# Top-k attention feeding a SoLU MLP on one core: constant rows and a tenth query tile in place of six small VectorE operations of a step, with a new table of places

## The chip, the core and the metric

The kernel runs on one core of a Trainium2 chip. Its engines are called PE (TensorE, the matmuls), DVE (VectorE), ACT (ScalarE), POOL (GpSimd) and SP (SyncE, which here only issues DMAs). Each engine works through its own instructions in order and waits on semaphores for the others. The metric is the device time of one execution in microseconds. A program is run several times; its time is the median. One execution is also taken by the profiler, and every row shown below comes from that one.

## The reference

Inputs are q, k and v of 8 batches x 8 heads x 576 positions x 64 columns, and the weights of an MLP (512 to 1024 to 512). For every query row only the scores that are at least as large as the 32nd largest of the row enter the softmax:

```python
scores = scale * np.matmul(q, k.transpose(0, 1, 3, 2))
kth = np.partition(scores, -top_k, axis=-1)[..., -top_k:-top_k + 1]
scores = np.where(scores >= kth, scores, -1000000000.0)
attn = np.exp(scores - max);  attn = attn / (sum(attn) + 1e-09)
x = (attn @ v), heads side by side: 4608 tokens x 512
h = x @ w_in
solu = h * softmax(h)
ln = (solu - mean) / sqrt(var + 1e-06) * g_ln
out = ln @ w_out
```

## The kernel before, in words

There are 32 steps, four for each batch. A step takes nine query tiles of 128 rows (`NT = 9`): four chunks with two heads each make tiles 0 to 7, and the last 64 positions of two heads together make tile 8. Groups of three tiles (`NG = 3`) share some small operations. For each tile the kernel finds the 32nd largest score by guessing thresholds. `spread` multiplies the queries with the second moments of the keys on PE; `spread_v` (L821 to L835) multiplies that with the queries on DVE and scales the means; `spread_r` adds it up to the expected spread of each row; `first_p` on POOL takes the square root and makes the gain `tb`; `first` makes the first threshold `t0`. `count0` counts the scores above it (DVE, two of nine on ACT in the first four steps), `second` moves the threshold, `count1` counts again (ACT; from the fifth step on tiles 7 and 8 on DVE), `third` moves it once more, and `count2` (ACT) leaves signs. `side`, `nearest`, `best` and `kth` (DVE) find the exact 32nd value among the eight nearest ones; `exps` is on ACT; `keep` (DVE, L1025) applies the mask and sums the row; `inverse` (L1030 to L1036) makes 1/sum for a group of three tiles; `norm` (POOL, L1040) scales the row by it. PE then transposes the tile (`transpose_p`), ACT copies it out of PSUM (`copy_p`), and `attn_v` multiplies with the values.

The MLP of a 128-token tile (a token) is spread over later steps: `mm1` (PE), `hexp` (ACT), `solu` (DVE), `square` (ACT), `ln` (POOL), `transpose_ln` (PE), `copy_ln` (ACT), `mm2` (PE), `store` (ACT copy, then a DMA from SP). Every eight steps there is one more token made of the tails of two batches.

The small operations that matter here. `moved` (L914 to L934) changes a threshold by (count + a) * `tb` * part + old. The two constants differ between tiles counted on DVE and tiles counted on ACT, so a step with both kinds issues four small operations: two of L926, two of L931. `spread_v` does each of its two operations twice, since tile 8 lies in another place of PSUM than tiles 0 to 7: L830 on 512 and on 64 columns, L833 on 8 and on 1. `inverse` adds 1e-9 (L1033) and then takes the reciprocal (L1036), three times in a step.

PSUM tiles called `big` hold scores, `spread`'s result (`y_ps`) and `mm1`'s result (`h_ps`); there are two such buffers, used in turn. The queries of a step lie in one buffer (`qm`), the keys' and queries' tails in two (`qk_tails`, in turn).

The order is written out by hand. Every piece of work gets a time in a table (`step_times` for step i at 39 i plus the entry, `early_times` for the first four steps, `key_times`, tables for tokens and weights), all pieces are sorted by it, and each engine and SP's DMA queue then follow that order. The numbers are places, not measured times: a step is 39 units of the table long.

At the start the MLP's weights come as 64-bit floats and are converted by DVE, ACT and POOL (`w_bits`, `w_low`, `w_mul`, `w_add`). Their exponents are checked again from a second load (`w_again`, `w_exp` on DVE, `w_check` on ACT); `w_passed` (L1218) adds up all checks, and `w_verdict` (L1225 to L1228) makes one flag, which every engine reads before it branches over a general version of the kernel.

Of the kernel before, what the change touches and what calls it, by code (L numbers as in the profile page):

```python
# [15 lines left out]
P = 128  # L16
# [427 lines left out]
def fast_path(  # L444
# [96 lines left out]
    g_rows = const.tile([NF, P], F32, tag="g_rows", name="g_rows")  # L541
    g_col = const.tile([P, NF], F32, tag="g_col", name="g_col")

    ok = const.tile([P, 6], F32, tag="ok", name="ok")
# [3 lines left out]
    qk_tails = [const.tile([P, 2, P], F32, tag=f"qk_tails{n}", name="qk_tails") for n in range(2)]  # L548
    v_diag = [const.tile([P, P], F32, tag=f"v_diag{n}", name="v_diag") for n in range(4)]
    for t in qk_tails + v_diag:  # L550
        nc.vector.memset(t, 0.0)
# [27 lines left out]
    def load_g():  # L579
        nc.sync.dma_start(out=g_rows, in_=moe_g_ln.rearrange("(c p) -> c p", p=P))  # L580
        tp = ps_tp.tile([P, NM, P], F32, tag="tp", name="tp_g")
        nc.tensor.transpose(tp[:, 0, 0:NF], g_rows, ident[0:NF, 0:NF])
        nc.scalar.copy(out=g_col, in_=tp[:, 0, 0:NF])
# [89 lines left out]
    def load_k(n):  # L673
# [9 lines left out]
        d["tails"] = qk_tails[n % 2]  # L683
        for h in range(2):
            hd = slice(h * ST, (h + 1) * ST)
            nc.sync.dma_start(out=d["tails"][hd, 0, hd], in_=q[b, 2 * hp + h, SM:S, :])
        nc.sync.dma_start(
            out=d["tails"][0:ST, 1, :].rearrange("p (h d) -> p h d", h=2),
# [29 lines left out]
    def prep_t(n):  # L718

        for m in range(2):  # L720
            nc.tensor.transpose(
                pre_of(n)[:, m * P : (m + 1) * P], ks[n]["tails"][:, m, :], ident
            )
# [44 lines left out]
    def load_q(i):  # L768
        b, chunks = steps[i]
        d = st[i]  # L770
        d["q"] = p1.tile([P, NT, D], F32, tag="qm", name="qm")
# [28 lines left out]
    def spread(i):  # L800
# [3 lines left out]
        d["ym"] = y[:, :, 0 : NM * (D + 1)].rearrange("p h (t e) -> p t h e", e=D + 1)  # L804
        d["yt"] = y[:, 0, NM * (D + 1) : (NM + 1) * (D + 1)]
        for c in range(NM):
            for h in range(2):
                hd = slice(h * D, (h + 1) * D)
                nc.tensor.matmul(
                    out=d["ym"][:, c, h, :], lhsT=trunc(queries_of(i, c)[hd, :]),  # L810
                    rhs=trunc(keys_of(i, c)["mom"][hd, :]), start=True, stop=True,
                )
        nc.tensor.matmul(
            out=d["yt"], lhsT=trunc(queries_of(i, NM)), rhs=trunc(keys_of(i, NM)["mom"]),
            start=True, stop=True,
        )

    def spread_v(i):
        d = st[i]
        ym, yt, q9 = d["ym"], d["yt"], d["q"]  # L820
        yq = d["yq"] = p2.tile([P, NT, D], F32, tag="w", name="yq")  # L821
        d["mean"] = small.tile([P, NT], F32, tag="mean", name="mean")
        for o, y, qq, mean in (
            (yq[:, 0 : 2 * NM, :].rearrange("p (t h) d -> p t h d", h=2), ym,
             q9[:, 0 : 2 * NM, :].rearrange("p (t h) d -> p t h d", h=2),
             d["mean"][:, 0 : 2 * NM].rearrange("p (t h) -> p t h", h=2)),
            (yq[:, 2 * NM, :], yt, q9[:, 2 * NM, :], d["mean"][:, 2 * NM : NT]),
        ):
            main = len(y.shape) == 4
            nc.vector.tensor_tensor(  # L830
                out=o, in0=y[:, :, :, 0:D] if main else y[:, 0:D], in1=qq, op=ALU.mult
            )
            nc.vector.tensor_scalar(  # L833
                out=mean, in0=y[:, :, :, D] if main else y[:, D : D + 1],
                scalar1=scale / SM, scalar2=None, op0=ALU.mult,  # L835
            )

    def spread_r(i):
        d = st[i]
        d["ss"] = small.tile([P, NT], F32, tag="ss", name="ss")  # L840
        nc.vector.tensor_reduce(out=d["ss"], in_=d["yq"], axis=AX.X, op=ALU.add)

    def first_p(i):
# [10 lines left out]
        )  # L854

    def first(i):
        d = st[i]
        d["t0"] = small.tile([P, NT], F32, tag="t0", name="t0")
        nc.vector.tensor_tensor(out=d["t0"], in0=d["mean"], in1=d["zs"], op=ALU.add)
# [81 lines left out]
    def third(i):  # L941

        n = NT - n1_of(i)
        moved(i, "n1", "t1", "t2", [(slice(0, n), -513.0, -0.25), (slice(n, NT), -31.5, 0.5)])
        d = st[i]
        t2 = d["t2"]
# [83 lines left out]
    def inverse(i, g):  # L1030
        js = slice(3 * g, 3 * g + 3)
        rden = columns(i, "rden")[:, js]
        nc.vector.tensor_scalar(  # L1033
            out=rden, in0=den_all[:, i, js], scalar1=1e-9, scalar2=None, op0=ALU.add
        )
        nc.vector.reciprocal(rden, rden)  # L1036
# [201 lines left out]
    def at(time, f, *args):  # L1238
# [4 lines left out]
        (load_q, [()], [-52.3]),  # L1243
        (prep_q, [()], [-25.66]),
        (prep_qc, [()], [-21.32]),
        (spread, [()], [-14.74]),
        (spread_v, [()], [-12.28]),
        (spread_r, [()], [-9.11]),
        (first_p, [()], [-5.94]),
        (first, [()], [-3.94]),  # L1250
        (scores, range(5), [-7.74, -5.46, -3.54, 0.79, 4.68]),
        (evac, range(9), [-4.99, -4.94, -2.71, -2.43, -0.91, -0.66, 1.75, 4.87, 8.58]),
        (count0, range(9), [-3.49, -3.39, -1.8, -1.65, 1.1, 2.22, 6.88, 7.72, 8.66]),
        (count1, range(9), [13.91, 15.21, 12.34, 15.17, 15.19, 16.89, 17.13, 16.96, 21.1]),
        (count2, range(9), [29.61, 24.17, 28.68, 23.34, 23.78, 23.94, 47.62, 27.29, 29.63]),
        (second, [()], [11]),
        (third, [()], [22.2]),
        (exps, range(5), [52.85, 51.89, 50.14, 56.99, 57.42]),
        (side, range(3), [37.21, 28.03, 49.2]),
        (inverse, range(3), [62.57, 64.96, 71.31]),  # L1260
        (count_off, [()], [50.83]),
        (kth, [()], [59.45]),
        (nearest, range(9), [41.07, 47.51, 39.3, 32.69, 29.76, 32.16, 57.74, 55.76, 51.21]),
        (best, range(9), [46.43, 52.3, 45.06, 36.45, 31.16, 33.82, 59.19, 58.14, 52.97]),
        (keep, range(9), [60.36, 61.34, 60.51, 62.49, 61.26, 61.16, 68.47, 62.8, 65.92]),
        (norm, range(9), [66.71, 64.69, 67.66, 72.59, 68.38, 72.61, 76.63, 77.78, 82.81]),
        (transpose_p, range(9), [
            70.08, 67.75, 72.27, 74.68, 72.98, 77.69, 79.24, 81.24, 83.57,
        ]),
        (copy_p, range(8), [71.1, 70.74, 73.88, 77.75, 75.87, 78.46, 81.22, 82.02]),  # L1270
        (copy_pt, [()], [84.44]),
        (transpose_last, range(2), [85.94, 86.48]),
        (copy_last, range(2), [87.65, 89.55]),
        (attn_v, range(2), [87.9, 90.3]),
        (copy_v, range(2), [90.37, 92.29]),
# [4 lines left out]
            (load_q, [()], [-111.2]),  # L1280
            (prep_q, [()], [-67.51]),
            (prep_qc, [()], [-54.3]),
            (spread, [()], [-19.53]),
            (spread_v, [()], [-17.76]),
            (spread_r, [()], [-17.34]),
            (first_p, [()], [-5.49]),
            (first, [()], [-3.33]),
            (scores, range(5), [-19.43, -18.9, -12.69, -4.58, 0.75]),
            (evac, range(9), [-15.83, -10.83, -8.96, -7.82, -7.17, -3.89, 2.47, 1.78, 4.92]),
            (count0, range(9), [4, -2, 3.06, 6.67, -2.83, -2.66, 5.03, 4.47, 9.4]),  # L1290
# [349 lines left out]
```

## Time and profile before

| what | us |
|---|---|
| median of 3 runs | 1291.85 (1290.74 to 1292.61) |
| the profiled execution's own time | 1289.73 |
| its span, first to last instruction | 1287.8 |
| PE busy in the span | 1184.2 |
| DVE busy | 1148.7 |
| ACT busy | 1130.6 |
| POOL busy | 481.1 |

The page of the profile has six parts; the first two give the busy time of each engine in all and in 40 equal slices of the span. A group row names a line, the engine, the tiles, the shape and the count, then the busy time in all and the mean of one in ns. A timeline row has a start, a duration and an instruction. The window view gives the busy time of each engine in a stretch.

`spread_r`, once in a step, marks the steps: in the trace it starts at 566.2, 601.3, 636.4, 671.5, 710.1, 746.5 and 788.2 us. Before the sixth one the steps are 23.7 to 41.2 us long, and from the eighth on the pattern 35.1 five times, then 38.6, 36.4 and 41.8, comes back.

### The profile page before, as it was taken

The page shows a single profiled execution, that of the slowest core. Times are in us where ns is not written, and L with a number is a line of the kernel's source. Part 1 is how long each engine was busy: PE and PEld are TensorE (multiplying, and loading weights), DVE is VectorE, ACT ScalarE, POOL GpSimd, SP SyncE. Part 2 cuts the span into 40 slices and gives each one's busy share as a digit, 9 for nine tenths or more (in the row PEclk, how much of TensorE's full clock was granted, in tenths as well). Part 3 has the DMA queues.
Part 4 walks back from the last instruction along what each step waited for, and adds up shares of the span by engine and source line. Part 5 has one row for each costly group of instructions (what it writes and reads, how often), then busy time and mean ns, then how long its engine had stood idle before and what let it go on. Part 6 is the DMA issues. An engine that isn't in the chain of part 4 may idle for free.

```text
span 1287.8 us, 19758 instructions
## 1 busy us (share of the span) xinstructions
PE 1184.2 (92%) x5955; PEld 672.1 (52%) x5955; DVE 1148.7 (89%) x2916; ACT 1130.6 (88%) x2478; POOL 481.1 (37%) x583
## 2 busy tenths in 40 slices
PE   6556789999999999999999999999999999998996
PEld 3334355555555555555555555555555555554543
DVE  5999989999999988999999988999999997999612
ACT  3989987999999989999999889999999889998634
POOL 5544533443432324444432234444333233443310
PEclk9668899999999999999999999999999999999998
DMA  7301111011111021011110011101110101102311
GB/s 224 98 26 38 52 33 42 19 31 37 39 37 27 20 55 38 27 31 29 47 37 23 24 46 37 37 22 32 51 37 18 31 25 39 30 7 74 131 58 61
DMA packets 106756, 56.97 MB, mean 44 GB/s; under 512 B 89736, under 2 KB 97936, under 8 KB 106640
## 3 DMA queue, kind: packets, MB, share of 16 engines
q1 hardware_dynamic: 106640, 55.61, 15.6%
q8 instruction: 50, 0.82, 0.3%
q14 instruction: 66, 0.54, 0.1%
HBM read 46.14 MB, written 9.44 MB: 43 GB/s over the span
## 4 chain that ended last, share of the span: by engine, by line
PE 44%; ACT 29%; DVE 19%; issue 4%; POOL 2%; DMA 1%; SPq 0%; DVEq 0%; ACTq 0%; POOLq 0%
PE s_ps L883 12%; PE o_ps L1199 10%; PE h_ps L1141 7%; PE tp_p L1054 7%; ACT junka L908 7%; ACT sg L960 6%; DVE E L1025 5%; DVE junkv L900 5%; ACT E L996 4%; DVE w L988 3%; PE om L1111 3%; ACT PT L1067 3%; DVE w L981 3%; PE tp_ln L1188 2%; ACT X L892 2%
## 5 line engine op out<-in xcount | busy, mean ns | idle before, releaser
L1199 PE MATMUL o_ps<-w_out,lnT 128*128 128x512 f32 x576 | 260.7, 596 | 0.0
L1040 POOL TENSOR_SCALAR E<-E,rden 128x576 f32<-128x576 f32 x256 | 204.2, 811 | 106.7 <-DVE rden L1036 80.2
L900 DVE TENSOR_SCALAR_CACHE_REDUCE junkv<-X,t 128x576 bf16<-128x576 f32 x280 | 224.3, 801 | 14.8 <-ACT X L892 6.6
L953 POOL TENSOR_SCALAR tt<-t 128x9 f32<-128x9 f32 x32 | 19.8, 619 | 561.7 <-DVE t L948 561.3
L1141 PE MATMUL h_ps<-w_in,xTm 128*128 128x512 f32 x512 | 226.8, 595 | 0.3 <-ACT xTm L1127 0.3
L883 PE MATMUL s_ps<-kT,qT 64*128 64x288 f32 x1024 | 200.7, 461 | 26.0 <-DVE mean L833 12.6
L981 DVE SCALAR_TENSOR_TENSOR w<-X,al,sg 128x576 f32<-128x576 f32 x256 | 213.3, 835 | 0.3
L988 DVE MAX8 w<-w 128x8 f32<-128x576 f32 x288 | 210.6, 750 | 0.2
L1025 DVE SCALAR_TENSOR_TENSOR E<-X,kth,E 128x576 f32<-128x576 f32 x256 | 200.4, 821 | 10.0 <-ACT E L996 9.4
L960 ACT ACTIVATE sg<-X,t 128x576 bf16<-128x576 f32 x256 | 196.8, 773 | 1.2 <-DVE t L948 1.2
L908 ACT ACTIVATE junka<-X,t 128x576 bf16<-128x576 f32 x232 | 180.5, 778 | 16.6 <-DVE t L931 12.6
L892 ACT ACTIVATE X<-s_ps 128x576 f32<-128x576 f32 x256 | 158.3, 655 | 34.6 <-PE s_ps L883 32.1
L1054 PE MATMUL tp_p<-ident,E 128*128 128x128 f32 x1024 | 153.4, 282 | 16.5 <-ACT PT L1067 6.8
L1067 ACT COPY PT<-tp_p 128x512 f32<-128x512 f32 x256 | 146.0, 597 | 20.0 <-PE tp_p L1054 19.7
L1199 PEld LDWEIGHTS o_ps<-w_out,lnT 128*128 128x128 f32 x576 | 104.7, 191 | 108.0 <-issue 107.9
L1054 PEld LDWEIGHTS tp_p<-ident,E 128*128 128x128 f32 x1024 | 114.7, 142 | 82.8 <-issue 36.9
L883 PEld LDWEIGHTS s_ps<-kT,qT 64*128 64x128 f32 x1024 | 116.8, 200 | 71.9 <-issue 27.8
L1141 PEld LDWEIGHTS h_ps<-w_in,xTm 128*128 128x128 f32 x512 | 94.8, 190 | 109.0 <-issue 102.9
L996 ACT ACTIVATE E<-X 128x1152 f32<-128x1152 f32 x128 | 147.2, 1177 | 0.0
L1111 PE MATMUL om<-PT,vm 128*64 128x256 f32 (+1 forms) x1024 | 141.2, 419 | 6.1 <-ACT xTt L1133 6.1
L1111 PEld LDWEIGHTS om<-PT,vm 128*64 128x64 f32 x1024 | 69.2, 139 | 64.9 <-issue 19.9
L850 POOL TENSOR_TENSOR zs<-zs,phalf 128x9 f32<-128x9 f32 x32 | 71.9, 2246 | 2.7
(127 smaller groups left out, 1651.3 us busy)
## 6 DMA issues: line engine op xcount, KB each, us to landing
km<-in_k_dram SPq DMA_DIRECT2D x32, 256.0 KB, 3.3
qm<-in_q_dram SPq DMA_DIRECT2D x128, 64.0 KB, 2.1
vm<-in_v_dram SPq DMA_DIRECT2D x32, 256.0 KB, 2.8
out_dram<-osb SPq DMA_DIRECT2D x32, 256.0 KB, 2.3
w_raw<-in_moe_w_in_dram SPq DMA_DIRECT2D x8, 512.0 KB, 5.5
w_raw<-in_moe_w_out_dram SPq DMA_DIRECT2D x8, 512.0 KB, 5.0
w_again<-in_moe_w_in_dram SPq DMA_DIRECT2D x8, 512.0 KB, 4.7
w_again<-in_moe_w_out_dram SPq DMA_DIRECT2D x8, 512.0 KB, 3.4
```

Of the source, the lines that this page charges most:

```text
L883: nc.tensor.matmul(out=big[h][:, half, 0:SH], lhsT=queries_of(i, t)[hd, :], rhs=kT[hd, k0 : k0 + SH], start=True, stop=True,)
L900: nc.vector.tensor_scalar(out=junk, in0=x_of(i, j), scalar1=st[i][t][:, j : j + 1], scalar2=None, op0=ALU.is_ge, op1=ALU.add, accum_out=co ...
L908: nc.scalar.activation(out=junk, in_=x_of(i, j), func=AF.Sign, scale=-1.0, bias=st[i][t][:, j : j + 1], accum_out=columns(i, c)[:, j : j + 1],
L960: nc.scalar.activation(out=d["sg", j], in_=x_of(i, j), func=AF.Sign, scale=-(1.0 + 2.0**-23), bias=d["t2"][:, j : j + 1], accum_out=column ...
L981: nc.vector.scalar_tensor_tensor(out=w, in0=x_of(i, j), scalar=d["al"][:, j : j + 1], in1=d.pop(("sg", j)), op0=ALU.subtract, op1=ALU.mult,)
L988: nc.vector.max(w8[:, j, :], st[i].pop(("w", j)))
L1025: nc.vector.scalar_tensor_tensor(out=e, in0=x_of(i, j), scalar=d["kth"][:, j : j + 1], in1=e, op0=ALU.is_ge, op1=ALU.mult, accum_out=den_a ...
L1040: nc.gpsimd.tensor_scalar(out=e, in0=e, scalar1=st[i]["rden"][:, j : j + 1], scalar2=1.0, op0=ALU.mult, op1=ALU.mult,)
L1054: nc.tensor.transpose(tp[:, c, :], e[:, c * P : (c + 1) * P], ident)
L1111: nc.tensor.matmul(out=o[h * D : (h + 1) * D, cols], lhsT=vm[:, h, c, :], rhs=pt[:, h * NM + c, :], start=(c == 0), stop=False,)
L1141: nc.tensor.matmul(out=h[:, half, :], lhsT=x[:, c, :], rhs=w_in[:, c, half * 512 : (half + 1) * 512], start=(c == 0), stop=(c == NP - 1),)
L1199: nc.tensor.matmul(out=o, lhsT=d["lnT"][:, c, :], rhs=w_out[:, c, :], start=(c == 0), stop=(c == NF - 1),)
```

## The change

- `n1_mid` and `n1_part` are constant rows with the two constants of each tile. `first_p` makes a second gain `tb2` = `tb` * `n1_part` on POOL, and `third` then needs three operations for all nine tiles in place of four, from the fifth step on.
- The query tile of a step, now the constant `q_all`, has a tenth tile of zeros. `spread` writes tile 8's product twice, the second one beside it, so that `spread_v` needs one operation of 640 columns and one of 10 in place of four.
- `inverse` takes the reciprocal alone; the 1e-9 is left out.
- `qk_tails` is one buffer in place of two; `g_rows` shares a buffer with the output.
- All tables of places are new. The verdict's work has earlier places: its last entry goes from 280.18 to 120.68, where the last token's second `mm2` half has 30 + 109.88 (before: 30 + 116.46).

```diff
+    for t, most, rest in ((n1_mid, 513.0, 31.5), (n1_part, -0.25, 0.5)):
+        n = NT - n1_of(FEW)
+        nc.vector.memset(t[:, 0:n], most)
+        nc.vector.memset(t[:, n:NT], rest)
+
+    q_all = const.tile([P, NT + 1, D], F32, tag="q_all", name="q_all")
+    nc.vector.memset(q_all[:, NT, :], 0.0)
...
-    qk_tails = [const.tile([P, 2, P], F32, tag=f"qk_tails{n}", name="qk_tails") for n in range(2)]
+    qk_tails = const.tile([P, 2, P], F32, tag="qk_tails", name="qk_tails")
...
-        d["q"] = p1.tile([P, NT, D], F32, tag="qm", name="qm")
+        d["q"] = q_all
...
-        nc.tensor.matmul(
-            out=d["yt"], lhsT=trunc(queries_of(i, NM)), rhs=trunc(keys_of(i, NM)["mom"]),
-            start=True, stop=True,
-        )
+        for h in range(2):
+            nc.tensor.matmul(
+                out=ym[:, NM, h, :], lhsT=trunc(queries_of(i, NM)),
+                rhs=trunc(keys_of(i, NM)["mom"]), start=True, stop=True,
+            )
...
+        nc.vector.tensor_tensor(
+            out=d["yq"].rearrange("p (t h) d -> p t h d", h=2), in0=ym[:, :, :, 0:D],
+            in1=d["q"].rearrange("p (t h) d -> p t h d", h=2), op=ALU.mult,
+        )
+        nc.vector.tensor_scalar(
+            out=d["mean"].rearrange("p (t h) -> p t h", h=2), in0=ym[:, :, :, D],
+            scalar1=scale / SM, scalar2=None, op0=ALU.mult,
+        )
...
+        if n1_of(i):
+            d["tb2"] = small.tile([P, NT], F32, tag="tb2", name="tb2")
+            nc.gpsimd.tensor_tensor(out=d["tb2"], in0=d["tb"], in1=n1_part, op=ALU.mult)
...
+            nc.vector.tensor_tensor(out=w, in0=d["n1"], in1=n1_mid, op=ALU.subtract)
+            nc.vector.tensor_tensor(out=w, in0=w, in1=d["tb2"], op=ALU.mult)
+            nc.vector.tensor_tensor(out=t2, in0=w, in1=d["t1"], op=ALU.add)
...
-        nc.vector.tensor_scalar(
-            out=rden, in0=den_all[:, i, js], scalar1=1e-9, scalar2=None, op0=ALU.add
-        )
-        nc.vector.reciprocal(rden, rden)
+        nc.vector.reciprocal(columns(i, "rden")[:, js], den_all[:, i, js])
...
     step_times = [
-        (load_q, [()], [-52.3]),
-        (prep_q, [()], [-25.66]),
-        (prep_qc, [()], [-21.32]),
-        (spread, [()], [-14.74]),
-        (spread_v, [()], [-12.28]),
-        (spread_r, [()], [-9.11]),
...
-        (scores, range(5), [-7.74, -5.46, -3.54, 0.79, 4.68]),
+        (load_q, [()], [-32.32]),
+        (prep_q, [()], [-23.58]),
+        (prep_qc, [()], [-19.16]),
+        (spread, [()], [-12.21]),
+        (spread_v, [()], [-7.24]),
+        (spread_r, [()], [-6.68]),
...
+        (scores, range(5), [-6.18, -4.89, -2.79, -0.19, 3.33]),
...
-        (load_k, [-151.18, -97.4, -60.66, -21.5], [-71.77, -54.35, -34.54, -26.23]),
+        (load_k, [-201.3, -72.25, -29.6, -11.15], [-102.79, -47.92, -20.27, -11.85]),
...
-        (prep_t, [-65.39, -32.79, -5.4, 17.24], [-50.7, -40.81, -7.18, 29.61]),
+        (prep_t, [-122.75, -35.92, -11.83, 12.83], [-60.15, -30.03, -13.35, 15.34]),
...
         (w_verdict, True, range(1), [
-            280.18,
+            120.68,
         ]),
```

## The prediction

> **What bounds the kernel now.** I first read the page's busy shares and slices. The second group of lines is the window view, one window to a step.
>
> ```profile
> PE 1184.2 (92%) x5955; PEld 672.1 (52%) x5955; DVE 1148.7 (89%) x2916; ACT 1130.6 (88%) x2478; POOL 481.1 (37%) x583
> ...
> PE   6556789999999999999999999999999999998996
> ...
> DVE  5999989999999988999999988999999997999612
> ...
> PEclk9668899999999999999999999999999999999998
> ```
>
> ```profile
> 114.80:156.10 41.30, 29.05 (x155) 16.43 (x155) 39.16 (x87) 38.24 (x91) 23.20 (x21) 0.93 0.23 62
> 601.30:636.40 35.10, 34.06 (x191) 20.02 (x190) 34.30 (x90) 34.10 (x78) 13.47 (x17) 1.00 0.20 51
> 636.40:671.50 35.10, 34.45 (x177) 19.50 (x177) 34.31 (x91) 33.43 (x73) 13.59 (x17) 1.00 0.13 35
> 671.50:710.10 38.60, 37.94 (x189) 21.02 (x186) 36.00 (x95) 36.10 (x78) 13.39 (x17) 1.00 0.11 27
> 710.10:746.50 36.40, 35.22 (x192) 20.89 (x191) 34.47 (x91) 33.02 (x75) 13.11 (x19) 1.00 0.09 23
> 746.50:788.20 41.70, 41.70 (x213) 23.59 (x212) 34.13 (x90) 35.68 (x80) 12.98 (x17) 1.00 0.19 48
> ```
>
> The columns are the window, its length, then busy us of PE, weight loads, DVE, ACT and POOL, and the granted clock. Three kinds of steps are seen. In a normal step (35.10 us, 16 of them) DVE is idle for 0.80 us only and sets the pace, but PE is idle for just 0.65 to 1.04 us and ACT for 1.00 to 1.67: whatever DVE gives back, PE can take up less than about 1 us of it. In the three steps that carry the tails' token (9 in all) PE is the limit, with 0.66, 1.18 and 0 us idle, and DVE is idle for up to 7.57. In the first six steps (window 114.8 is one) DVE also converts weights; it is idle for 2.14 of 41.30 us, ACT for 3.06, and PE is far from full, at a clock of 0.93 there and lower in the slices before.
>
> **What the change removes.** DVE's small operations, from the groups by line, and one stretch of the timeline (DVE's rows, then POOL's):
>
> ```profile
> L830 DVE TENSOR_TENSOR yq<-y_ps,qm 128x512 f32<-128x512 f32 x64 | 28.6, 453 | 9.0 <-PE y_ps L813 8.2
> L1033 DVE TENSOR_SCALAR rden<-den_all 128x3 f32<-128x3 f32 x96 | 23.7, 247 | 0.1
> L1036 DVE RECIPROCAL rden<-rden 128x3 f32<-128x3 f32 x96 | 16.9, 177 | 3.3
> L833 DVE TENSOR_SCALAR mean<-y_ps 128x8 f32<-128x8 f32 x64 | 9.7, 151 | 0.0
> ```
>
> ```profile
> 632.33 0.08 DVE L1160 DVE_READ_ACCUMULATOR solu<-h_ps,rs,e_sb 128x1 f32 x1
> 632.45 0.15 DVE L1164 TENSOR_SCALAR nmu<-nmu 128x1 f32<-128x1 f32 x1
> 632.52 0.49 DVE L1033 TENSOR_SCALAR rden<-den_all 128x3 f32<-128x3 f32 x1
> 633.04 0.18 DVE L1036 RECIPROCAL rden<-rden 128x3 f32<-128x3 f32 x1
> ```
>
> ```profile
> 631.53 1.46 POOL L1040 TENSOR_SCALAR E<-E,rden 128x576 f32<-128x576 f32 x2
> ```
>
> *The 1e-9 of `inverse`.* L1033 takes 247 ns in the mean and 0.035 passes before L1036 may start: 0.28 us, three times a step, 0.84 us. The 0.49 us row is one of 25 long ones: it ends with POOL's E at 632.99. [...] L1036, which started beside a running POOL operation about 33 times, never took over 179 ns[...]. [...] only 0.20 x 3 = 0.60 is saved; I take 0.84 and keep 0.60.
>
> *`spread_v`.* L830 moves on after 608 ns (512 columns) and 132 ns (64): 1.06 ns a column, so 640 columns take 608 + 136 = 744 against 740. Merging saves nothing, since the zeros cost what the second start did. [...] The second L833 moves on after 65 ns: 0.07 saved.
>
> *`third`.* Its four operations now pass DVE in 78, 121, 83 and 192 ns (start to start, 627.07 to 627.54), because each pair is independent. The three new ones are a chain. A dependent small operation follows after 0.205 (L926 to L931 at 617.19), so 3 x 0.205 = 0.62; and in the new order `count1` of tile 8 stands directly before, whose count it reads, which costs 0.12 as at 632.33 to 632.45. 0.73 against 0.47: **0.26 lost**, though one operation is gone. [...] a `norm` (0.74 us) queued on POOL could stop each of them. But POOL's order is `norm` 0, then `tt`, which needs `third`'s result, then `norm` 2 and 1: only `norm` 0 can collide, and it runs beside `count1`[...]. Bounds 0 to 0.74; I take 0.
>
> *Moved collisions.* `side` of tiles 0 to 2 was stopped for 0.49 us a step (0.64 against 0.15 at 608.53, ending with POOL's L1040). In the new order it comes behind the third reciprocal, while POOL runs `first_p`, beside which no DVE row was long (-0.49); `side` of tiles 3 to 5 comes after a `keep`, just when `norm` 4 has its scale (+0.49). Together 0; the table may miss by 0.5 either way.
>
> So DVE's saving is 0.84 + 0.07 - 0.26 = **0.65 us** in a normal step (0.1 to 1.1).
>
> **What it adds elsewhere.** PE gets one 65-column matmul with its weights a step (L813: 209 ns, 98 ns for the load, overlapped): 0.05 to 0.3, I take 0.1. POOL gets `tb2` (nearest: L852, 257 ns) behind `tb`; POOL is busy 13.5 of 35.1 us and only later `norm`s stand behind it: 0. DVE's start gains four tiny memsets and one of 64 columns and loses one of 256: 0. The single `qk_tails` holds SP at the third load of a batch until `prep_t` of the one before (places -11.85 and -13.35); SP's next pieces are the store (1.16) and `load_q` (6.68): covered. `load_q`'s six DMAs take 3.0 us to issue (1.92 + 1.11 at 564.0) and 2.1 to land, and `prep_q` comes 8.7 units (7.9 us at 35.1 us to 39) later: covered by 2.8 us; without that PE would wait, and the spread, `first` and all counts with it. In the first six steps SP's order puts one more 512 KB weight chunk ahead of the queries: up to 2 us late, with DVE converting a chunk more meanwhile: 0.
>
> **The end.** The last matmul ends at 1277.86, and the verdict trails it:
>
> ```profile
> 1277.90 0.58 ACT L1206 COPY osb<-o_ps 128x512 f32<-128x512 f32 x1 [2.13 <-PE o_ps L1199]
> ...
> 1278.51 1.14 SPq L1208 DMA_DIRECT2D out_dram<-osb  x2
> ...
> 1279.86 0.19 ACT L642 ACTIVATION_READ_ACCUMULATOR junka<-w_exp,m 128x1 f32 x1
> ...
> 1281.43 0.14 DVE L1228 TENSOR_SCALAR bad<-n_ok 1x1 int32<-1x1 f32 x1
> ```
>
> From the flag (1281.57) to the end of the span are 6.2 us (every engine reads it, PE's branch alone takes 3.66). With the verdict placed ahead of the last `mm2` this begins on PE at the last matmul, and on SP when the output is issued (1279.65). The output lands 2.3 later, at 1282.0, and the closing semaphores take 1.9: end at 1283.9 in place of 1287.8, **3.9 us**. 16 `w_exp` (0.43) and 16 `w_check` (0.9) move forward into stretches where DVE and ACT are half idle (slices "61" and less): 0.
>
> **The sum.** In normal steps of the 0.65 us I let 0.45 through: PE's and ACT's idle 0.65 to 1.7 leaves room, but three engines at 95% or more hand work round. 16 x 0.45 = 7.2. In tails' steps only PE's idle time (1.84 in three) can go: 1.0 for each of three groups, less 9 x 0.1 for the matmul: 2.1. The first six steps: `third` is unchanged in four of them, so 0.9 saved on DVE, against ACT close behind and weights in the way: 0.4 x 6 = 2.4. End 3.9. Sum 15.6. The profiled execution took 1289.73 and would take 1274.1; the runs' median stands 2.1 above it: **1276**. The table of places as such I put at zero: the orders show neither sign.
>
> **The rivals.**
> A. *The table is worth something of its own*: PE's idle time is used up. Normal steps fall to PE's 34.2 + 0.1, 0.8 x 16 = 12.8; tails' steps lose 1.5 in each group, 4.5; the first six 1.0 each, 6; end 3.9: 27, so 1265. For it: DVE was idle 18.8 us in the first six steps.
> B. *PE or ACT is the bound at once* and steps stay as they are; only the end counts: 1288. For it: PE at 97 to 98% in normal steps. Against: PE's idle time there ends on ACT and DVE.
> C. *Slower: the scores wait for `spread_v`.* `spread`'s result holds one of two `big` buffers until DVE's `mean` is done. The first `scores` stood 4.5 units behind `spread_v`; now 1.1, with three `keep`s and a `side` ahead of it on DVE. The wait exists:
>
> ```profile
> PE s_ps L883 <- DVE mean L833: 12.6, 4, 7.3
> ```
>
> Four waits of 32 before. All of PE's later work and so ACT's copies queue behind such a wait. If DVE is late by 1.5 us in each of 25 steps, 0.9 of it replaces idle time and 0.6 is lost: +15, with 3.9 and 2.4 kept: 1301. It decides from 1.15 us (0.9 + 6.3/25). Against: the first `count0` moved back as well (-3.49 to 0.99), and in tails' steps DVE is early.
> D. *The saving doesn't come about*[...]: 0.25 less a step, 1281; inside the forecast's range.
>
> **How the numbers follow.** Forecast 0.50 (own range 1268 to 1284, D within it), A 0.22 (1255 to 1268), B 0.16 (1284 to 1290), C 0.12 (1290 to 1310). About 0.2% (2.6 us) is what a measurement can tell from no change. Faster: 0.50 + 0.22 + 0.13 of B = 0.85; same: 0.03 of B + 0.02 of C = 0.05; slower 0.10. Cutting A at 1262 leaves out 0.1 and C above 1290 about 0.1: 1262 to 1290.
>
> **What would show it.** L1033 gone, L1047's reciprocals at 177 ns; one row of 640 columns near 830 ns; three `third` rows, each about 0.2 us after the other; normal steps near 34.65 us with DVE still under 1 us idle; the `bad` row ahead of the last `mm2` and the span ending about 6 us behind the last matmul. Wrong if PE's waits on `mean` grow to tens of us, if `prep_q` waits for its DMA, or if POOL's `norm` rows stop `third`.

## The result

The kernel after takes **1277.38 us** (median of 4 runs, 1275.48 to 1279.52) against 1291.3 (1290.65 to 1292.61) of the kernel before, run beside it: ratio 0.9891, 95% interval 0.9871 to 0.9912, so 1.1% faster. The prediction was 1276 with the range 1262 to 1290.

The page of the kernel after, busy times and slices:

```profile
PE 1196.7 (94%) x5987; PEld 678.2 (53%) x5987; DVE 1115.1 (87%) x2732; ACT 1128.8 (88%) x2478; POOL 505.5 (40%) x611
...
PE   5657789999999999999999999999999999999997
...
DVE  5689989999998979999998979999999979999721
...
PEclk9998889999999999999999999999999999999999
```

DVE has lost 33.6 us of busy time and PE has gained 12.5 (9.8 of them stand in e2 as well, which has the new places but not the additional matmul). The window view, one window to a step (length, then PE, weight loads, DVE, ACT, POOL, clock):

```profile
600.10:635.00 34.90, 34.46 (x191) 19.84 (x190) 33.60 (x85) 34.01 (x79) 13.63 (x18) 1.00 0.20 51
635.00:669.30 34.30, 33.99 (x174) 19.24 (x172) 33.45 (x84) 33.37 (x74) 14.49 (x18) 1.00 0.12 34
669.30:708.90 39.60, 39.60 (x195) 22.09 (x194) 34.66 (x88) 36.08 (x77) 13.93 (x18) 1.00 0.09 24
708.90:743.70 34.80, 34.68 (x193) 20.71 (x192) 33.09 (x84) 32.98 (x75) 15.24 (x20) 1.00 0.11 28
743.70:786.30 42.60, 42.36 (x213) 23.52 (x212) 33.56 (x84) 35.57 (x82) 13.55 (x18) 1.00 0.19 48
```

A normal step has fallen from 35.08 to 34.39 us (mean of five) and all three engines are now within 1.3 us of full in it. The three steps with a tails' token have not fallen: 38.6 + 36.4 + 41.8 = 116.8 before, 117.0 now. Read by `spread_r`'s starts, the profiled spans divide as follows (us; the runs of the later sections stand beside them; "step" is the mean of the five normal steps 13 to 17, "3 tails" the sum of a group of tails' steps):

| kernel | start to step 0 | steps 0 to 6 | steps 6 to 31 | step | 3 tails | step 31 to end | median |
|---|---|---|---|---|---|---|---|
| before | 18.5 | 219.8 | 912.3 | 35.08 | 116.8 | 137.2 | 1291.3 |
| after | 23.0 | 217.9 | 902.9 | 34.39 | 117.0 | 133.9 | 1277.4 |
| e2, places alone | 21.9 | 215.9 | 903.7 | 34.42 | 117.1 | 133.8 | 1278.0 |
| e3, no 1e-9, old places | 18.8 | 219.4 | 906.9 | 34.62 | 117.1 | 137.3 | 1284.0 |
| e10, one `side` earlier | 19.3 | 220.1 | 907.6 | 34.75 | 116.7 | 137.2 | 1285.8 |
| e12, three edits, old places | 19.9 | 219.2 | 903.8 | 34.45 | 117.4 | 135.4 | 1277.8 |
| e5, after, `third` in four | 22.4 | 215.0 | 900.9 | 34.27 | 117.3 | 132.8 | 1273.0 |

The profiled execution of the kernel after (1279.52) was the longest of its four: its first step took 19.0 us (mean granted clock of the execution 0.986), as in the profiles of e9 and e13 (19.0 us, 0.988), where those of e4 to e8, which keep its places too, have 15.9 to 16.4 us (0.964 to 0.967), and why is open. So the two profiles show a gain of only 10.1 us (along the row a loss of 4.5, then gains of 1.9, 9.4 and 3.3), where the medians show 13.9.

DVE's small rows after the change, from its groups by line and shape (busy us in all, mean ns, idle before):

```profile
L1039 DVE SCALAR_TENSOR_TENSOR Et<-Xt,kth,Et 128x576 f32<-128x576 f32 x32 | 34.3, 1071 | 0.0
L834 DVE TENSOR_TENSOR yq<-y_ps,q_all 128x640 f32<-128x640 f32 x32 | 26.0, 812 | 1.9 <-PE y_ps L824 1.9
L983 DVE SCALAR_TENSOR_TENSOR al<-n,tt 128x3 f32<-128x3 f32 x96 | 16.7, 174 | 31.0 <-ACT sg L974 31.0
L1047 DVE RECIPROCAL rden<-den_all 128x3 f32<-128x3 f32 x96 | 16.1, 168 | 0.1
L838 DVE TENSOR_SCALAR mean<-y_ps 128x10 f32<-128x10 f32 x32 | 4.9, 153 | 0.0
```

and the same two rows of the kernel before that the prediction did not show:

```profile
L969 DVE SCALAR_TENSOR_TENSOR al<-n,tt 128x3 f32<-128x3 f32 x96 | 27.6, 287 | 0.4 <-ACT sg L960 0.2
L1025 DVE SCALAR_TENSOR_TENSOR Et<-Xt,kth,Et 128x576 f32<-128x576 f32 x32 | 27.4, 857 | 0.0
```

`side` (`al`) has become shorter with the same operation, from 287 to 174 ns, and the `keep` of tile 8 (`Et`) longer, from 857 to 1071 ns. No edit touches either operation. That is the first sign that the new order, and not only the edits, is at work.

### The profile page after: what moved, and what is told of

Same layout as the page of the kernel before. It is cut to its first block, busy times and chain, and to the rows that moved or that the text cites. A ratio compares the mean times of both kernels' runs of the same rounds, so it can differ in the third digit from the quotient of the medians.

```text
span 1277.7 us, 19653 instructions
## 1 busy us (share of the span) xinstructions
PE 1196.7 (94%) x5987; PEld 678.2 (53%) x5987; DVE 1115.1 (87%) x2732; ACT 1128.8 (88%) x2478; POOL 505.5 (40%) x611
## 4 chain that ended last, share of the span: by engine, by line
PE 49%; ACT 34%; DVE 11%; issue 4%; SPq 1%; DMA 1%; DVEq 0%; ACTq 0%
PE s_ps L891 12%; PE o_ps L1210 11%; PE h_ps L1152 10%; ACT sg L974 7%; ACT junka L916 7%; PE tp_p L1065 5%; PE om L1122 5%; ACT E L1010 4%; ACT PT L1078 4%; DVE junkv L908 3%; ACT X L900 3%; DVE E L1039 3%; PE tp_ln L1199 2%; PE om L1126 2%; ACT e_sb L1181 1%
## 5 line engine op out<-in xcount | busy, mean ns | idle before, releaser
L1051 POOL TENSOR_SCALAR E<-E,rden 128x576 f32<-128x576 f32 x256 | 233.8, 924 | 533.5 <-DVE rden L1047 282.5
L891 PE MATMUL s_ps<-kT,qT 64*128 64x288 f32 x1024 | 207.5, 463 | 20.0 <-ACT X L900 11.5
L916 ACT ACTIVATE junka<-X,t 128x576 bf16<-128x576 f32 x232 | 183.1, 789 | 5.2 <-DVE t L939 1.0
L891 PEld LDWEIGHTS s_ps<-kT,qT 64*128 64x128 f32 x1024 | 120.4, 200 | 69.3 <-ACT X L900 30.4
L1010 ACT ACTIVATE E<-X 128x1152 f32<-128x1152 f32 x128 | 152.9, 1197 | 0.0
L855 POOL TENSOR_TENSOR zs<-zs,phalf 128x9 f32<-128x9 f32 x32 | 59.2, 1850 | 2.7
L908 DVE TENSOR_SCALAR_CACHE_REDUCE junkv<-Xt,t 128x576 bf16<-128x576 f32 x56 | 45.3, 809 | 15.4 <-ACT Xt L900 15.0
```

Source lines behind the costliest of these rows:

```text
L891: nc.tensor.matmul(out=big[h][:, half, 0:SH], lhsT=queries_of(i, t)[hd, :], rhs=kT[hd, k0 : k0 + SH], start=True, stop=True,)
L908: nc.vector.tensor_scalar(out=junk, in0=x_of(i, j), scalar1=st[i][t][:, j : j + 1], scalar2=None, op0=ALU.is_ge, op1=ALU.add, accum_out=co ...
L916: nc.scalar.activation(out=junk, in_=x_of(i, j), func=AF.Sign, scale=-1.0, bias=st[i][t][:, j : j + 1], accum_out=columns(i, c)[:, j : j + 1],
L1051: nc.gpsimd.tensor_scalar(out=e, in0=e, scalar1=st[i]["rden"][:, j : j + 1], scalar2=1.0, op0=ALU.mult, op1=ALU.mult,)
```

## The experiments

Most of them set the theory of the prediction against the rival that the table of places carries the gain. The kernel before was run again beside each of them and gave 1290.5 to 1291.5; the kernel after was not, so that a difference to it can be off by about 1 us.

### The places alone, and the 1e-9 in the old places

e2 has the operations of the kernel before, and all tables of places of the kernel after; two entries of the many:

```diff
-        (spread_v, [()], [-12.28]),
+        (spread_v, [()], [-7.24]),
...
-            280.18,
+            120.68,
```

> The kernel before with the changed kernel's tables of places and none of its other edits. Theory (DVE's own time sets the normal steps, and the edits' DVE saving is what shortens them): normal steps stay near 35.1 us, the end is 3.3 us shorter and the start some 4 us later as in the changed kernel's trace, so about 1291, within 3 us of before. Rival (the new places carry the gain): 1282 or less.

Measured: 1278.01 (1277.08 to 1279.02), ratio 0.9901 (0.9881 to 0.9921). The theory fell here: nearly the whole gain is there without one edit of an operation. In e2's groups the two rows of `inverse` are still there, but the first one is hardly ever stopped any more, and neither is `side`, while `keep` of tile 8 is:

```profile
L1025 DVE SCALAR_TENSOR_TENSOR Et<-Xt,kth,Et 128x576 f32<-128x576 f32 x32 | 34.7, 1084 | 0.0
L969 DVE SCALAR_TENSOR_TENSOR al<-n,tt 128x3 f32<-128x3 f32 x96 | 17.6, 184 | 27.4 <-ACT sg L960 27.0
L1033 DVE TENSOR_SCALAR rden<-den_all 128x3 f32<-128x3 f32 x96 | 16.0, 167 | 0.1
```

(L1033 was 247 ns before.) Counted in rows that are lengthened beside a POOL operation: L1033 from 25 of 96 to 1, `al` from 24 of 96 to 7, `Et` from 3 of 32 to 21. On DVE, start to next start, a step changes by -0.34 (L1033), -0.43 (`al`), -0.22 (`first`), -0.11 (reciprocals), -0.10 (`best`), +0.42 (`Et`), +0.03 (`nearest`): -0.75, and the step by 0.66.

e3 is the counterpart, one edit in the old places. It leaves the 1e-9 out, as the kernel after does:

```diff
-        nc.vector.tensor_scalar(
-            out=rden, in0=den_all[:, i, js], scalar1=1e-9, scalar2=None, op0=ALU.add
-        )
-        nc.vector.reciprocal(rden, rden)
+        nc.vector.reciprocal(rden, den_all[:, i, js])
```

> The kernel before, with only the addition of 1e-9 in inverse removed (the output lacks that 1e-9). Theory: L1033 costs 0.28 us three times a step with what POOL holds up, so 0.84 us of DVE go; PE's idle time of 0.65 to 1.75 lets most of it through in the 16 normal steps: 34.3 to 34.5 us each, 1278 to 1282 in all. Rival ([...] PE and ACT are the bound at once): 34.9 us or more a step, 1287 to 1291.

Measured: 1284.03 (1282.8 to 1284.63), ratio 0.9942 (0.9922 to 0.9962): 7.5 us. L1033 had taken 0.93 us of DVE in a step; the step fell by 0.46, so half of it passed. The reciprocal alone is never lengthened (0 of 96). Rows of `al` and `nearest` are, 50 in place of 43, but that is worth only 0.06 us in a normal step. The other half DVE spends waiting: `first` now stands idle for POOL's square root,

```profile
L859 DVE TENSOR_TENSOR t<-mean,zs 128x9 f32<-128x9 f32 x32 | 6.6, 207 | 11.8 <-POOL zs L850 11.8
```

where it waited 0.3 us for it in the kernel before; in a normal step that is 0.40 us.

The mirror of e3 puts the 1e-9 back into the kernel after:

```diff
-        nc.vector.reciprocal(columns(i, "rden")[:, js], den_all[:, i, js])
+        rden = columns(i, "rden")[:, js]
+        nc.vector.tensor_scalar(
+            out=rden, in0=den_all[:, i, js], scalar1=1e-9, scalar2=None, op0=ALU.add
+        )
+        nc.vector.reciprocal(rden, rden)
```

> The changed kernel with the addition of 1e-9 put back. Theory: 0.2 to 0.28 us three times a step come back on DVE: normal steps rise from 34.4 to 35.0 to 35.2, 10 to 13 us in all, 1287 to 1291. Rival (the new places hide it or carry the gain): 1277 to 1281.

Measured: 1284.27 (1281.79 to 1288.07), ratio 0.9945 (0.9932 to 0.9959): 6.9 us worse than after. The operation is worth about the same in both orders, though in the new one it only costs DVE 0.59 a step.

So two things are true at once: the places alone bring 13 us, and the removal of the 1e-9 brings 7 more in the new places. Since the whole change brings 14, the other edits must cost some 6 there. The next two runs look for them.

### `third` and `spread_v`

e5 is the kernel after with `third` as it was before, without `tb2`:

```diff
-            d["tb2"] = small.tile([P, NT], F32, tag="tb2", name="tb2")
-            nc.gpsimd.tensor_tensor(out=d["tb2"], in0=d["tb"], in1=n1_part, op=ALU.mult)
...
-            nc.vector.tensor_tensor(out=w, in0=d["n1"], in1=n1_mid, op=ALU.subtract)
-            nc.vector.tensor_tensor(out=w, in0=w, in1=d["tb2"], op=ALU.mult)
-            nc.vector.tensor_tensor(out=t2, in0=w, in1=d["t1"], op=ALU.add)
+        moved(i, "n1", "t1", "t2", [(slice(0, n), -513.0, -0.25), (slice(n, NT), -31.5, 0.5)])
```

> The changed kernel with third in its old four operations and without tb2 on POOL. By the ledger of DVE's time in a normal step the chain of three costs 0.34 us more than the four did, and 0.18 go in the wait for the count in front of it. Theory (DVE still sets the normal steps): 34.39 falls by 0.3 or more, 16 normal steps give 5 us: 1271 to 1273. Rival (PE with 0.2 to 0.6 and ACT with 0.9 us idle are the bound by now): 34.2 or more a step, 1275 to 1277.

Measured: **1272.97** (1272.72 to 1273.25), ratio 0.9857 (0.9842 to 0.9872): 4.4 us better than the kernel after, with one operation more. Its timeline on DVE:

```profile
622.34 0.08 DVE L905 DVE_READ_ACCUMULATOR junkv<-Xt,t 128x1 f32 x1
622.34 0.28 DVE L931 SCALAR_TENSOR_TENSOR step<-n,tb 128x7 f32<-128x7 f32 x2
622.54 0.28 DVE L936 SCALAR_TENSOR_TENSOR t<-step,t 128x7 f32<-128x7 f32 x2
622.86 0.17 DVE L953 TENSOR_SCALAR t<-t 128x9 uint32<-128x9 uint32 x1
```

and that of the kernel after:

```profile
626.71 0.08 DVE L908 DVE_READ_ACCUMULATOR junkv<-Xt,t 128x1 f32 x1
626.90 0.17 DVE L957 TENSOR_TENSOR step<-n,n_mid 128x9 f32<-128x9 f32 x1
627.10 0.17 DVE L958 TENSOR_TENSOR step<-step,tb 128x9 f32<-128x9 f32 x1
627.31 0.17 DVE L959 TENSOR_TENSOR t<-step,t 128x9 f32<-128x9 f32 x1
627.51 0.17 DVE L962 TENSOR_SCALAR t<-t 128x9 uint32<-128x9 uint32 x1
```

Four operations pass in 0.52 us, since the second of each pair needs nothing of the first (a row "x2" of 0.28). Three pass in 0.61, one every 0.205, and they begin 0.19 behind the accumulator's read, whose count the first one subtracts; the pair for tiles 0 to 6 does not need that count and begins at once.

The chain is not all that e5 takes away. `tb2` stands ahead of five `norm`s on POOL and makes each of them 0.27 us later. In the kernel after, POOL's rows and the `nearest` beside the last of them are

```profile
604.07 0.20 POOL L862 TENSOR_TENSOR tb<-tb,n_part 128x9 f32<-128x9 f32 x1
604.36 2.91 POOL L1051 TENSOR_SCALAR E<-E,rden 128x576 f32<-128x576 f32 x4
607.24 0.75 POOL L1051 TENSOR_SCALAR Et<-Et,rden 128x576 f32<-128x576 f32 x1
607.55 1.05 DVE L995 SCALAR_TENSOR_TENSOR w<-X,al,sg 128x576 f32<-128x576 f32 x1
```

and in e5, at the same place of the step:

```profile
602.59 0.74 POOL L1042 TENSOR_SCALAR Et<-Et,rden 128x576 f32<-128x576 f32 x1
603.17 0.81 DVE L986 SCALAR_TENSOR_TENSOR w<-X,al,sg 128x576 f32<-128x576 f32 x1
```

The `nearest` that begins 0.44 us before the end of POOL's row is lengthened, the one that begins 0.16 before it is not. Of the 25 steps from the seventh on it is long in 19 in the kernel after and in e6, and in 22 in e4, which all have `tb2`; in e2, e5 and e9, which do not, it is long in 3. That is 0.23 us of DVE in a normal step, as much as the chain costs, and no run parts the two.

Of the 6 us, 4.4 are found with e5 by the medians. Its profile shows less of it, since that of the kernel after is the long one: steps 6 to 31 are 2.0 shorter and the end 1.1. For the rest there is no run.

e6 is the kernel after with `spread` and `spread_v` as before:

```diff
-        for h in range(2):
-            nc.tensor.matmul(
-                out=ym[:, NM, h, :], lhsT=trunc(queries_of(i, NM)),
-                rhs=trunc(keys_of(i, NM)["mom"]), start=True, stop=True,
-            )
+        nc.tensor.matmul(
+            out=d["yt"], lhsT=trunc(queries_of(i, NM)), rhs=trunc(keys_of(i, NM)["mom"]),
+            start=True, stop=True,
+        )
...
```

> The changed kernel with spread_v in its old four operations and without the second product of tile 8 on PE; the tenth tile stays unused. Theory: the row of 640 columns (0.734) and that of 10 (0.075) stand for 0.739 and 0.138, so DVE loses 0.07 us a step and PE gains back 0.1 at most: 1276.5 to 1279, no difference that can be measured. Rival (fewer starts count for more than their rows show, by the waits around them): 1281 or more.

Measured: 1276.31 (1276.17 to 1279.67), ratio 0.9889 (0.9873 to 0.9905). The step is 34.42 against 34.39. The merge is worth nothing that can be measured, in either direction.

### Is it moved collisions? One entry of the old table

e10 is the kernel before but for one number:

```diff
-        (side, range(3), [37.21, 28.03, 49.2]),
+        (side, range(3), [32.5, 28.03, 49.2]),
```

> The kernel before, with the one entry for `side` of tiles 0 to 2 in the table of a step moved from 37.21 to 32.5; no operation and no other entry is changed. If single moved collisions make the gain of the new places, the L983 row of tiles 0 to 2 leaves the reach of POOL's row E<-E,rden, 0.49 us of DVE less in a step, and with half to all of it passed on in 16 to 25 steps the median falls by 3 to 8 us: 1283 to 1288. If the collision only moves to the next DVE operation with two SBUF inputs, or if the moved row now waits for ACT's count2, the median stays at 1290 to 1293.

(L983 is the line in the kernel after; here it is L969.) Measured: 1285.77 (1285.45 to 1286.1), ratio 0.9961 (0.9947 to 0.9975), **5.0 us** for one entry. The timeline of the kernel before, DVE's row and POOL's rows beside it:

```profile
608.53 0.64 DVE L969 SCALAR_TENSOR_TENSOR al<-n,tt 128x3 f32<-128x3 f32 x1
...
606.96 1.48 POOL L1040 TENSOR_SCALAR E<-E,rden 128x576 f32<-128x576 f32 x2
608.40 0.76 POOL L1040 TENSOR_SCALAR Et<-Et,rden 128x576 f32<-128x576 f32 x1
```

The row of 3 columns ends at 609.17, with POOL's at 609.16. In e10:

```profile
602.71 0.18 DVE L1036 RECIPROCAL rden<-rden 128x3 f32<-128x3 f32 x1
602.80 0.13 DVE L969 SCALAR_TENSOR_TENSOR al<-n,tt 128x3 f32<-128x3 f32 x1
602.85 0.81 DVE L981 SCALAR_TENSOR_TENSOR w<-X,al,sg 128x576 f32<-128x576 f32 x1
```

Lengthened `al` rows fall from 24 to 4, DVE gains 0.50 in a step, the step falls by 0.33. Nothing else was stopped in exchange: L1033 has 24 long rows (25 before), and those of `nearest` fall from 19 to 14. Which kinds are stopped at all, the trace of the kernel before shows by the rows that start while one of POOL's `norm` rows is under way. With two tensors read from SBUF, 23 of 29 `al` are over 0.1 us longer than the median of their kind, 11 of 11 `nearest`, 3 of 5 `keep` and 3 of 4 `first`; with one, 25 of 27 of L1033, but none of 86 counts (0.815 us at most), of 30 `MAX8` (0.762) and of 32 reciprocals (0.178).

### The end

In e7 the kernel after gets back the old entries of `w_again`, `w_exp`, `w_check`, `w_passed` and `w_verdict`:

```diff
-            113.61, 115.1, 85.29, 102.12, 110.42, 108.77,
+            215.56, 235.59, 242.57, 269.1, 243.49, 241.78,
...
-            120.68,
+            280.18,
```

> The changed kernel with the old places of the second weight load, its checks and the verdict alone. Theory: the flag comes behind the last output again and PE's read and branch start 3 to 4 us later: 1280 to 1282. Rival (the end is set by the last output's landing or by PE's last matmul anyway): 1277 to 1278.

Measured: 1284.24 (1282.33 to 1286.9), ratio 0.9949 (0.993 to 0.9969), 6.9 us worse, more than either theory had. The last tokens' work has other places now, and the late verdict ends further behind it than in the kernel before: the last output is issued at 1269.47, and

```profile
1276.06 0.15 DVE L1238 TENSOR_REDUCE n_ok<-tp_ok 1x1 f32<-1x6 f32 x1 [0.38 <-PE tp_ok L1236]
```

is 6.6 behind it (2.7 in the kernel before: 1281.24 against 1278.51). So 6.9 is the price of these old places among the new ones, not the worth of the move in the kernel before. That is what e11 asks, the kernel before with the new entries of the same five, but two of `w_passed` a few places later:

```diff
-            215.56, 235.59, 242.57, 269.1, 243.49, 241.78,
+            113.61, 115.1, 85.29, 116.12, 117.42, 108.77,
...
-            280.18,
+            120.68,
```

> The kernel before, with only the entries of w_again, w_exp, w_check, w_passed and w_verdict of the kernel after (two entries of w_passed, 102.12 and 110.42, become 116.12 and 117.42, since the last token's squares are summed later in the old places). If the verdict's place is worth what the prediction put on it, the span ends 3 to 4 us sooner after the last matmul and the median is 1287 to 1288.5. If the moved checks cost the last steps as much as the end gives back, it stays at 1290.5 to 1292.5.

Measured: 1289.27 (1287.96 to 1293.56, 21 runs), ratio 0.9986 (0.9977 to 0.9994): 1.5 us, between the two. In its profile, which is that of the longest of the 21 executions, the time from the last output's issue to the end falls from 9.3 to 6.7, but that issue comes 1.6 later after step 31 than before. That fits checks which now lie in the last tokens' stretch, but no run separates it.

### Three edits in the old places

e12 takes the kernel before with e3, e10 and e11 together (the 1e-9 is left out):

```diff
-        nc.vector.tensor_scalar(
-            out=rden, in0=den_all[:, i, js], scalar1=1e-9, scalar2=None, op0=ALU.add
-        )
-        nc.vector.reciprocal(rden, rden)
+        nc.vector.reciprocal(rden, den_all[:, i, js])
...
-        (side, range(3), [37.21, 28.03, 49.2]),
+        (side, range(3), [32.5, 28.03, 49.2]),
...
-            280.18,
+            120.68,
```

> The kernel before with three edits in its old places: no 1e-9 (left out, so the quotient is without it), `side` of tiles 0 to 2 earlier, the verdict's entries of e11. If the parts add up (7.3 for the 1e-9, 3 to 8 for `side`, 3 to 4 for the end), 1273 to 1278, as low as the kernel after without its new table for the rest. If PE and ACT stop it once DVE is relieved, so that the parts overlap, 1279 to 1284.

Measured: 1277.83 (1277.4 to 1280.17), ratio 0.9899 (0.9884 to 0.9914). The single gains, 7.5 + 5.0 + 1.5 = 14.0, add up nearly: 13.0 are measured. The old table, with one entry of a step and the verdict's work moved and one operation less, is as fast as the kernel after. Its windows:

```profile
598.90:634.50 35.60, 34.25 (x192) 20.12 (x191) 33.37 (x88) 34.31 (x78) 13.80 (x18) 1.00 0.19 49
634.50:668.40 33.90, 33.52 (x170) 19.13 (x170) 32.98 (x87) 32.89 (x72) 12.71 (x17) 1.00 0.14 38
668.40:707.40 39.00, 38.63 (x193) 21.50 (x192) 34.61 (x92) 36.71 (x79) 13.39 (x17) 1.00 0.10 26
```

Three of five normal steps are at 33.9, with PE idle for 0.4, and a fourth is at 34.8; the fifth (35.6) and the tails' steps (117.4) are longer than before and take up part of that gain.

### The start, and where it stops

In the kernel after, the first `spread_r` comes 4.5 us later; one weight chunk ahead of the queries was a suspect. e8 moves it back behind them:

```diff
-            -276.46, -242.91, -119.89, -48.24, -39.11, -108.23, -12.14, 20.55, -14.8, 3.35,
+            -276.46, -242.91, -119.89, -48.24, -39.11, -38.23, -12.14, 20.55, -14.8, 3.35,
```

> The changed kernel with one weight chunk of 512 KB (the sixth) loaded behind the second keys in place of ahead of the first queries. Theory: the first spread result comes 2 to 4 us earlier (it was at 23.0 against 18.5 before the change), and all later steps with it: 1273.5 to 1275.5. Rival (the weights' conversion on DVE and the clock set the pace of the first six steps, so an early first step is given back): 1276.5 to 1278.5, with the sixth step starting no earlier.

Measured: 1275.39 (1274.24 to 1277.01), ratio 0.9876 (0.9859 to 0.9893). Step 0 comes 1.0 earlier; the intervals of the two kernels overlap, so a worth of 0 to 2 us stays open. e9 has this entry and e5's `third` in four operations:

> Both: third in four operations and the chunk later. Theory: the two gains add, 1268 to 1271. Rival: neither counts, 1275 to 1278.

Measured: 1272.35 (1271.44 to 1275.45), ratio 0.985 (0.9836 to 0.9863), not to be told from e5.

The last run asks whether moving one more collision still pays. It takes e5 and moves `spread_v` between the `side` and the `keep` of tile 8 that POOL lengthens:

```diff
-        (spread_v, [()], [-7.24]),
+        (spread_v, [()], [-8.02]),
```

> The kernel after with `third` in four operations (as in the run with that edit alone, 1272.97), and one more entry changed: `spread_v` in the table of a step from -7.24 to -8.02. Its product[...] then stands between the `side` and the `keep` of tile 8 that POOL's E<-E,rden lengthens from 0.81 to 1.23 us in 20 of 32 steps. If DVE's stopped operations still set the pace, `keep` is back at 0.81, at most 0.42 us in a step less a wait of about 0.25 for PE's y_ps; with half of 0.2 to 0.4 passed on in 16 steps the median falls by 1.5 to 3.5: 1269.5 to 1271.5. If PE is the limit by now (0.03 to 0.61 us idle in a normal step), or if the stop moves to the `nearest` behind it, it stays at 1272 to 1274.

Measured: 1273.2 (1271.89 to 1276.34), ratio 0.9859 (0.9838 to 0.988): nothing, against e5. Its groups (in e5 the two means are 835 and 1072 ns):

```profile
L986 DVE SCALAR_TENSOR_TENSOR w<-X,al,sg 128x576 f32<-128x576 f32 x256 | 216.6, 856 | 0.2
L1030 DVE SCALAR_TENSOR_TENSOR Et<-Xt,kth,Et 128x576 f32<-128x576 f32 x32 | 27.2, 849 | 0.0
```

`keep` of tile 8 is back at its length (3 long rows in place of 20), -0.34 us a step, and `nearest` is longer by 0.36 a step (36 rows over 0.9 us in place of 13). It is not the `nearest` right behind that `keep`, which stays at 0.81, but the one behind `spread_r`. DVE comes to it earlier than before, while POOL is still at a row of `ln`:

```profile
599.38 1.19 POOL L1183 TENSOR_SCALAR solu<-solu,nmu,rstd 128x1024 f32<-128x1024 f32 x1
600.23 0.94 DVE L986 SCALAR_TENSOR_TENSOR w<-X,al,sg 128x576 f32<-128x576 f32 x1
```

So the place given to `spread_v` took one collision away and made another.

Not run: `third` in three operations, or the merged `spread_v`, in the old places.

## Why the prediction was right, and where it was not

**The total was right and its largest cause was not named.** The step that failed is the last line of the sum: "The table of places as such I put at zero: the orders show neither sign", and with it "Together 0" for the moved collisions. The places alone carry about 13 of the 13.9 us (e2). That is the premise of rival A, but not its result: A had DVE's early idle time and all of PE's used up, 1265, and only the step time and the end came. That 1276 lies so near to 1277.4 is luck in part: terms that were too high and one that was left out made up for each other.

**Moved collisions.** The prediction weighed two of them, -0.49 and +0.49. The first was right (`side` of tiles 0 to 2, and e10 shows it to be worth 5.0 us by itself). The second did not come where it was expected: `side` of tiles 3 to 5 slips through in 0.16 us, and the `keep` behind it is stopped in its place:

```profile
631.53 0.16 DVE L983 SCALAR_TENSOR_TENSOR al<-n,tt 128x3 f32<-128x3 f32 x1
631.60 1.23 DVE L1039 SCALAR_TENSOR_TENSOR Et<-Xt,kth,Et 128x576 f32<-128x576 f32 x1
...
630.99 1.24 POOL L1051 TENSOR_SCALAR E<-E,rden 128x576 f32<-128x576 f32 x1 [0.52 <-DVE rden L1047]
```

(The timeline of the kernel after; the last row is POOL's and ends at 632.23.) What was not counted at all: the new places take L1033's stops away even where the operation stays (-0.34), and those of `first` (-0.22), and `tb2` brings one of `nearest` (+0.23). The prediction looked at how the rows that it had seen long would move, and not at the other kinds of which some were long already (19 of 288 `nearest`, 7 of 288 `keep` and 3 of 32 `first`, by over 0.1 us) or at L1033 in the new order.

**L1033** was sized right, 0.84 against 0.93 measured on DVE in the old order, and the bare reciprocal stayed as short as L1036 had been: none of 96 was lengthened in e3, and in the kernel after none took over 0.177 us. But 0.34 of it is a gain that the new places make anyway; it cannot be counted for both. Of DVE's gain half passed in the old places (0.46 of 0.93), 0.6 in the new (0.37 of 0.59); the prediction had 0.69. Rival D, in which other rows take the saving back, hardly came: in e3 seven more rows of other operations were stopped, for 0.06 us in a normal step. e10 and e13 show how much depends on where an operation stands: 5.0 us in e10 for one entry, and in e13 0.34 us of a step gained on one row and 0.36 lost on another.

**`third`** was right in its own rows: 0.26 lost on DVE, 0.23 measured (0.615 for three and 0.41 behind the counts' reads, against 0.51 and 0.29 in e5). No `norm` stopped it: in the groups of the kernel after each of the three rows has a mean of 170 ns, as argued, and the counts that start beside a `norm` there, 118 of them, take 0.816 us at most, against a mean of 0.80. But `tb2`, which belongs to it, was put at 0 because "only later `norm`s stand behind it", and that failed: those `norm`s come later by it, and the last one runs into a `nearest`. The edit so costs DVE about 0.46 us a step, not 0.26.

**`spread_v`** right: the 640 columns move on after 0.734 against 0.739 for the two, the second `mean` had cost 0.063 (0.07). The merge of the two products so saved 0.005. In e6 no worth of the merge, with the PE matmul that it needs, can be measured.

**The shape of the sum.** For steps 6 to 31 the prediction had 7.2 + 2.1 = 9.3, and the profile shows 9.4. That is luck, since the two terms were both off: sixteen normal steps gave 10.2, and the tails' steps lost 0.3 in each group where 0.7 (1.0 less 0.3 for the matmul) was to be gained. PE's idle time in a normal step, too, was read from two of the five: over all five of the kernel before it is 0.37 to 1.75 us, not 0.65 to 1.04. In every run in which normal steps fell by 0.4 or more the tails' steps grew by 0.3 to 0.8 (table above and e13's 117.6). In the new places PE is full there (0 to 0.25 us idle), which fits that it has no room for what a faster DVE hands on; in e12's old places it is idle for up to 1.2 us in such a step, so that this reason is not enough.

**The start** was put at zero and cost 4.5 us up to the first `spread_r`. PE does the first scores ahead of `spread` there, and ACT copies them only behind a weight conversion whose chunk lands at 19.8; `spread` has to wait for that copy (1.8 us, 0.7 in e8) and begins at 21.5. The six steps after it give back 1.9 in this profile and 4.0 to 5.0 in the runs with the same places, so that 2.4 of gain became something between a loss of 2.6 and a gain of 0.9. e8 shows only a part of it to be the chunk; the rest stays open.

**The end**: 3.9 forecast, 3.3 measured from step 31 on; the move alone gave 1.5 in the old places (e11). The flag is ready 11 us before the last output is issued, as said:

```profile
1260.08 0.15 DVE L1238 TENSOR_REDUCE n_ok<-tp_ok 1x1 f32<-1x6 f32 x1 [8.17 <-PE tp_ok L1236]
1260.26 0.14 DVE L1239 TENSOR_SCALAR bad<-n_ok 1x1 int32<-1x1 f32 x1
...
1270.62 0.59 ACT L1217 COPY osb<-o_ps 128x512 f32<-128x512 f32 x1 [5.57 <-PE o_ps L1210]
...
1271.23 1.14 SPq L1219 DMA_DIRECT2D out_dram<-osb  x2
```

The span ends 6.5 behind that issue, where 5.4 was forecast (1283.9 against 1278.51). The output is not what is late: its last packet ends at 1273.8, 1.4 behind the end of the issue where 2.3 was reckoned. It is SP itself: it reads the flag only when it has issued the output (1272.42, 0.79 us), branches at 1273.3 and goes on at 1275.81, and in between lie two packets of instructions. The view of DMA from 1273.9 to 1275.0:

```profile
DMA packets 2, 0.02 MB, mean 15 GB/s; under 512 B 0, under 2 KB 0, under 8 KB 0
...
q14 instruction: 2, 0.02, 5.4%
```

The prediction had counted this branch for PE (3.66) and let SP wait for the output alone. The closing after it takes the forecast 1.9.

**Covered as said**: no `prep_q` waits for its load after the start, and rival C's wait became smaller, not larger; in the waits of the kernel after (us, times, longest)

```profile
PE s_ps L891 <- DVE mean L838: 5.0, 2, 3.0
```

stands against 12.6 before. Rival B fell with e3: DVE's relief passes at about half. The prediction let 0.69 of it through and gave PE and ACT as the reason for the rest; in e3 it is DVE's own wait for POOL. In e5 and e13 PE is idle for only 0.03 to 0.6 us in a normal step, so its bound is near; that a further 0.34 us off one DVE row brought nothing in e13 does not prove it, since another row took 0.36 back.

## What to carry to other kernels

Before an edit of operations is costed, count the rows that are longer than their own kind beside another engine's, in both orders: one entry of a table, which took a 3-column operation out of POOL's reach, was worth 5 us, two thirds of a whole operation removed from every group. A stop that is taken away can come back elsewhere (e13), and an operation added on an engine with time to spare moves all rows behind it (`tb2`), so look at what those rows then run beside, and read the gain from a run of the order alone. And count start to next start, not operations: three small operations in a chain took longer (0.61 us) than four in independent pairs (0.52), and undoing that edit, with its `tb2`, gave 1273.0, 1.4% under before.

## What the runs showed of the hardware that was not expected

- A DVE operation of 3 columns in 128 rows and two SBUF inputs took 0.64 us in place of 0.16 when it stood beside POOL's 0.76 us row, and ended within 0.01 us of it (the kernel before, 608.53). None of the 32 reciprocals (0.178 us at most) and 30 `MAX8` (0.762) that started beside a `norm` row was lengthened. The 0.16 us `al` at 631.53 ran while a POOL row of the same kind was under way (630.99 to 632.23), so being beside one is not enough; POOL's row was itself 1.24 us long there in place of 0.76. It had begun inside a `keep` (630.81 to 631.61); what held it up is not shown.
- A `nearest` of 576 columns that began 0.43 to 0.46 us before the end of POOL's row took 1.04 us in place of 0.81; one that began 0.15 to 0.19 before it took 0.81 (the kernel after, e4, e5).
- In the rows of `third` a dependent operation started 0.205 us after the one before it (the kernel after, 626.90 to 627.51), an independent one 0.08 to 0.12 after (the kernel before, 627.07 to 627.35); the operation that reads a count started 0.19 behind the start of the accumulator's read (the kernel after, 626.71), one that does not need it at the same time (e5, 622.34).
- SP went on 2.5 us after its branch (3.7 in the kernel before), with two packets of instructions between (the kernel after, 1274.2). There it stands behind the last output, and the span ends 1.9 us later.
